# A hand-ordered two-stage kernel: the steps behind the 178th in another order, four of them on another engine

## The chip, the cores and the metric

The kernel runs on one core of a Trainium2 chip. The metric is the device time of one execution in microseconds (us); lower is better. The core has engines that each work through their own queue of instructions in order: TensorE (PE, matrix multiplication), VectorE (DVE), ScalarE (ACT), GpSimd (POOL) and SyncE (SP), which here only issues transfers. Between engines there are semaphores: an instruction waits until what it reads has been written, or until the buffer that it writes has been read for the last time.

## The reference

Attention by polynomial sketches, then a layer whose activation is a quotient of polynomials, on 4 batches of 4 heads, 1088 tokens, 32 per head:

```python
def phi(x):
    a = np.einsum('rd,bhsd->bhsr', S1, x)
    b = np.einsum('rd,bhsd->bhsr', S2, x)
    return np.einsum('bhsi,bhsj->bhsij', a, b).reshape(*x.shape[:-1], r * r)
q_p, k_p = (phi(q), phi(k))
kv = np.einsum('bhsf,bhsd->bhfd', k_p, v)
z = np.sum(k_p, axis=2)
num = np.einsum('bhsf,bhfd->bhsd', q_p, kv)
den = np.einsum('bhsf,bhf->bhs', q_p, z)[..., None] + 1e-06
...
h = x @ w_in                      # x: num / den, (4352, 128); w_in: (128, 2048)
P = a[0] + a[1] * h + a[2] * h2 + a[3] * h3
Q = 1.0 + np.abs(b[0]) * np.abs(h) + np.abs(b[1]) * h2
g = P / (Q + 1e-06)
return (g @ w_out).astype(np.float32)
```

## The kernel before

Nothing in the kernel is scheduled by the compiler: the instructions of every engine stand in the order in which the program issues them, and that is the order of the string `ORDER`, 650 steps. A loop at the end of the kernel splits each step at its points, looks up a function by its first letters and calls it; a last `.a` puts the step on ScalarE, `.d` on VectorE. Moving a step in the string moves its instructions in its engine's queue and changes when its buffers are taken. Each tile belongs to a group of a fixed number of buffers, and a new one takes a buffer whose last reader has come.

The first stage works on keys (`K`, batch.what) and queries (`Q`, batch.part.what). For keys: `T` transpose (VectorE, line 299), `s` sketches (TensorE, 306), `c` copy of one sketch out of PSUM, `f` features (VectorE, 318), `p` products with the values (TensorE, 337), `k` copy of the result (into kvz). For queries: `T` transpose, `sk` sketches (TensorE, 373), `c` copy, `dw` and `dr` write to and read back from memory (issued by SP, 399 to 410), `f` features (VectorE, 417), `p` numerator and denominator (TensorE, 433), `pl` denominator plus 1e-6 (442 on VectorE, 445 on ScalarE), `r` reciprocal (VectorE, 450), `x` quotient (VectorE, 455), `b` three transposes back (TensorE, 461), `kk` copy into xT, the second stage's input.

The second stage has 21 units, each of 256 or 512 tokens by 4, 8 or 16 blocks of 128 hidden columns; most are 128 x 4096 values, units 18 to 20 are 128 x 2048 and twice 128 x 1024. A unit's steps:

- `H` hidden layer in parts of 1024 (TensorE, 518, 32-bit) and `E` its evacuation from PSUM as bf16 into hh (line 272 on ScalarE, 274 on VectorE). Two PSUM buffers serve all H.
- the denominator: `U` absolute value (531; on ScalarE 529), `W` scale and bias (539; on ScalarE 537), `Y` product (554), all VectorE. In units 6, 8, 10, 12 and 14 ScalarE's `D` (544) takes the square instead of W and Y, and `M`, a transfer issued by GpSimd (550), joins u to it.
- `L` logarithm (ScalarE, 576) and `X` exponential (ScalarE, 581): the reciprocal r, in two buffers.
- the numerator: `P` (VectorE 559, ScalarE 562), `V` (VectorE, 572); in units 7, 9 to 15 `A` adds a constant from memory, by a transfer that GpSimd issues (568). `S` (VectorE, 585) multiplies hh and r, `G` (VectorE, 589) S and the numerator. Units 16 and 17 have `B` and `C` (594, 601) instead.
- `Or`, `Os`, `Og`, `Om`, `On` (TensorE, 618): products with the second weights, summed in one PSUM accumulator; all units of the same tokens share it. `ST` (ScalarE, 272; the last, ST20, on VectorE and ScalarE, 633 and 635) empties it, and only then can the next tokens begin. `OUT` stores (SP, 655).

`w6` and `w7` make scaled copies of the second weights for units 16 and 17, in memory that the key features k_p have left (lines 678 on VectorE, 680 on ScalarE). `F` loads the next batch's q, k or v, `AW` writes the constant for A to memory, `Z` are idle matmuls.

Of the kernel before, what the change touches and what calls it, by code (L numbers as in the profile page):

```python
# [770 lines left out]
```

## Time and profile before

| | us |
|---|---|
| median of 3 runs (254.99 to 255.8) | 255.01 |
| the profiled execution's own time | 255.07 |
| its span, first to last instruction | 253.3 |
| TensorE busy, 2603 matmuls | 244.4 |
| VectorE busy, 229 instructions | 240.1 |
| ScalarE busy, 179 instructions | 231.9 |
| GpSimd busy, 59 instructions | 32.9 |

The time is 1.8 us longer than the span; what lies around the span belongs to the program's start and end. Busy times of one engine can't be added over instructions: on VectorE and ScalarE each instruction begins a little before the one in front has ended, unless it waits for something. In lists of groups a row has line, engine, operation, out<-in with shapes, count, busy us and mean ns of one. In timelines a row has start, duration, engine, line, and in brackets idle time ahead and what ended it; equal neighbours are merged into one row.

### The profile page before, as it was taken

To read this page: it belongs to the slowest core of one execution; us is meant where nothing else is said; L and a number is where in the kernel's file an instruction comes from. 1 tells how busy PE (TensorE), PEld (TensorE's weight loads), DVE (VectorE), ACT (ScalarE), POOL (GpSimd) and SP (SyncE) were. 2 spreads that over 40 slices of the span, in tenths; PEclk is the share of its full clock that TensorE was granted. 3 is DMA by queue.
4 is the path that set the end of the run, shared out by engine and by line. 5 is a ranking of instruction groups with operands and counts; after the bars stand their busy time and mean duration, and the time that the engine had idled before them with its cause. 6 is when DMAs were issued, how large, how long until landed. Compare 5 with 4: busy or idle time off the path is not lost.

```text
span 253.3 us, 6086 instructions
## 1 busy us (share of the span) xinstructions
PE 244.4 (96%) x2603; PEld 172.1 (68%) x2606; DVE 240.1 (95%) x229; ACT 231.9 (92%) x179; POOL 32.9 (13%) x59
## 2 busy tenths in 40 slices
PE   7999899999999999999999999899999999999983
PEld 3777645665576667666676677565757589999883
DVE  3798999999999999999999999999999999999993
ACT  2179989998999999999999999999999999999990
POOL 4030000000003000420040700620125200000000
PEclk9999999999999999999999999999999999999999
DMA  6998475407925487599028992799187991000111
GB/s 180 278 333 187 146 242 179 129 6 238 215 70 114 91 185 225 115 207 194 5 63 190 177 204 42 138 161 213 30 168 129 212 211 34 0 3 3 41 47 39
DMA packets 22458, 34.47 MB, mean 136 GB/s; under 512 B 2976, under 2 KB 14880, under 8 KB 22432
## 3 DMA queue, kind: packets, MB, share of 16 engines
q0 software_dynamic: 3744, 13.63, 29.2%
q1 hardware_dynamic: 18400, 20.38, 28.8%
q8 instruction: 20, 0.33, 0.5%
q10 hardware_dynamic: 288, 0.08, 0.1%
q14 instruction: 6, 0.05, 0.1%
HBM read 25.10 MB, written 3.74 MB: 114 GB/s over the span
## 4 chain that ended last, share of the span: by engine, by line
PE 38%; ACT 21%; DVE 19%; issue 13%; DMA 6%; SPq 1%; ACTq 0%; DVEq 0%
PE h_ps L518 20%; PE out_ps L618 10%; ACT r L581 6%; ACT ln L576 6%; ACT hh L272 5%; DVE g L589 3%; DVE w L554 3%; DMA v_sb<-in_v_dram 3%; DVE s L585 3%; PE att_ps L337 3%; PE att_ps L433 2%; DVE g L594 2%; DVE g L572 2%; DMA k_sb<-in_k_dram 2%; DVE w L539 2%
## 5 line engine op out<-in xcount | busy, mean ns | idle before, releaser
L518 PE MATMUL h_ps<-xT,w_in_sb 128*128 128x512 f32 (+1 forms) x320 | 128.4, 538 | 0.2 <-DMA w_in_sb<-in_moe_w_in_dram 0.2
L518 PEld LDWEIGHTS h_ps<-xT,w_in_sb 128*128 128x128 f32 x320 | 56.8, 190 | 36.4 <-issue 31.9
L272 ACT CAST hh<-h_ps 128x1024 bf16<-128x1024 f32 x66 | 65.9, 1044 | 2.0 <-PE h_ps L518 1.9
L581 ACT ACTIVATE r<-ln 128x4096 bf16<-128x4096 f32 (+2 forms) x21 | 63.1, 3004 | 0.5 <-PE out_ps L618 0.5
L576 ACT ACTIVATE ln<-w 128x4096 f32<-128x4096 bf16 (+2 forms) x16 | 44.9, 2803 | 0.0
L585 DVE TENSOR_TENSOR s<-hh,r 128x4096 bf16<-128x4096 bf16 (+2 forms) x21 | 39.4, 1879 | 0.2 <-ACT r L581 0.2
L618 PEld LDWEIGHTS <-r 128*128 128x128 bf16 x544 | 31.8, 98 | 8.8 <-issue 8.3
L618 PEld LDWEIGHTS <-g 128*128 128x128 bf16 x544 | 31.7, 98 | 7.2 <-issue 5.6
L618 PE MATMUL out_ps<-w_out,r 128*128 128x128 bf16 x544 | 33.7, 219 | 1.5 <-ACT out_sb L272 1.5
L589 DVE TENSOR_TENSOR g<-g,s 128x4096 bf16<-128x4096 bf16 (+2 forms) x19 | 34.7, 1837 | 0.1
L572 DVE TENSOR_TENSOR g<-g,hh 128x4096 bf16<-128x4096 bf16 (+2 forms) x19 | 34.7, 1834 | 0.0
L618 PE MATMUL out_ps<-w_out,g 128*128 128x128 bf16 x480 | 29.8, 219 | 0.1
L550 POOL DMA_DIRECT2D w<-u x10 | 12.3, 1359 | 133.3 <-ACT w L544 74.2
L554 DVE TENSOR_TENSOR w<-w,u 128x4096 bf16<-128x4096 bf16 (+2 forms) x16 | 28.0, 1750 | 0.1
L618 PEld LDWEIGHTS <-s 128*128 128x128 bf16 x352 | 20.6, 98 | 5.3 <-issue 4.0
L531 DVE TENSOR_SCALAR u<-hh 128x4096 uint16<-128x4096 uint16 (+2 forms) x20 | 20.9, 1047 | 0.8 <-ACT hh L272 0.8
L576 ACT ACTIVATE ln<-w,scale 128x4096 f32<-128x4096 bf16 x5 | 18.8, 3759 | 0.0
L544 ACT ACTIVATE w<-hh,root 128x4096 bf16<-128x4096 bf16 x5 | 18.6, 3726 | 0.1
L568 POOL DMA_DIRECT2D g<-ones x16 | 15.6, 1240 | 22.7 <-DVE g L572 13.0
L559 DVE TENSOR_SCALAR g<-hh,a_k 128x4096 bf16<-128x4096 bf16 (+2 forms) x16 | 18.5, 1168 | 0.0
L618 PE MATMUL out_ps<-w_out,s 128*128 128x128 bf16 x288 | 18.2, 219 | 0.0
L539 DVE TENSOR_SCALAR w<-u,b_abs 128x4096 bf16<-128x4096 bf16 (+2 forms) x15 | 16.6, 1106 | 0.0
(92 smaller groups left out, 194.5 us busy)
## 6 DMA issues: line engine op xcount, KB each, us to landing
g<-ones POOLq DMA_DIRECT2D x16, 512.0 KB, 9.6
w<-u POOLq DMA_DIRECT2D x10, 512.0 KB, 6.0
a_all<-sk_d SPq DMA_DIRECT2D x6, 352.0 KB
b_all<-sk_d SPq DMA_DIRECT2D x12, 176.0 KB
v_sb<-in_v_dram SPq DMA_DIRECT2D x12, 144.0 KB
k_sb<-in_k_dram SPq DMA_DIRECT2D x3, 544.0 KB
q_sb<-in_q_dram SPq DMA_DIRECT2D x3, 544.0 KB
out_dram<-out_sb SPq DMA_DIRECT2D x19, 64.0 KB
```

Of the source, the lines that this page charges most:

```text
L272: nc.scalar.copy(out=out, in_=in_)
L518: nc.tensor.matmul(t[:, (x - part * m) * tl:(x - part * m + 1) * tl], lhsT=w_in_sb[:, (f0 + x) * 128:(f0 + x + 1) * 128], rhs=xT[:, p:p + ...
L531: nc.vector.tensor_scalar(out=at(i, "u", *c).bitcast(U16), in0=at(i, "hh", *c).bitcast(U16), scalar1=0x7FFF, scalar2=None, op0=AX.bitwise_and)
L539: nc.vector.tensor_scalar(out=at(i, "w", *c), in0=at(i, "u", *c), scalar1=ab1, scalar2=ab0, op0=AX.mult, op1=AX.add)
L544: nc.scalar.activation(out=at(i, "w", *c), in_=at(i, "hh", *c), func=ACT.Square, scale=root)
L554: nc.vector.tensor_mul(out=at(i, "w", *c), in0=at(i, "w", *c), in1=at(i, "u", *c))
L572: nc.vector.tensor_mul(out=at(i, "g", *c), in0=at(i, "g", *c), in1=at(i, "hh", *c))
L576: nc.scalar.activation(out=ln_sb[:, :ce - c], in_=at(i, "w", c, ce), func=ACT.Ln, bias=1.0 + 1e-6, scale=scale0 if i in SQ else 1.0)
L581: nc.scalar.activation(out=at(i, "r", c, ce), in_=ln_sb[:, :ce - c], func=ACT.Exp, scale=-1.0)
L585: nc.vector.tensor_mul(out=at(i, "s", *c), in0=at(i, "hh", *c), in1=at(i, "r", *c))
L589: nc.vector.tensor_mul(out=at(i, "g", *c), in0=at(i, "g", *c), in1=at(i, "s", *c))
L618: nc.tensor.matmul(outs[t0][:, m * 128:(m + 1) * 128], lhsT=z[:, m * 128:(m + 1) * 128], rhs=w, start=first and j == 0 and m == 0, stop=le ...
```

## The change

Only the string differs. The first 178 steps stay as they are; behind them the same steps stand in another order. Four steps have another engine: `Q2.1.pl` and `w7` go from ScalarE to VectorE, `U19` too, and `Q3.0.pl` goes from VectorE to ScalarE. GpSimd's steps keep their order among themselves; those of the four other engines change places.

```diff
-Q1.2.dw Q1.1.dr K2.s1 Q0.3.p X2.0 E4.0.a P3.1.a H4.2 Q0.3.pl.d K2.c1.d Q1.0.f Q2.0.c.a V3.0 Q0.3.r Og1.0 E4.1.a L3.0
-Q1.0.p Q1.0.pl.a H4.3 Os1.0 Q1.0.r Q0.3.x E4.2.a Q0.3.b Q1.0.x Q1.0.b Q1.2.dr Or2.0 S2.0 E4.3.a Q0.3.kk.a Q1.0.kk.a
-H5.3 X3.0 U4.0.d H5.2 E5.2.a K2.f1 Q1.1.f Q2.2.sk Q1.1.p Q1.1.pl.a G2.0 Q2.1.sk Q2.1.c.a E5.3.a Q2.0.dw W4.0.d H5.0
-Og2.0 H5.1 Q1.1.r Y4.0 E5.0.a Or1.0 L4.0 E5.1.a H6.2 Os2.0 Q1.1.x Q1.2.f S3.0 Q2.2.c.a H6.3 ST2.a E6.2.a E6.3.a F3.q
-Q1.1.b Q1.1.kk.a Q3.0.T H6.1 X4.0 Q2.1.dw H6.0 F3.k E6.0.a Q1.2.p F2.v Q1.2.pl.a K2.p0 K2.p1 Q3.2.T P4.0.d U5.0.d
-Q2.0.dr Q3.1.T W5.0.d H7.0 V4.0 Y5.0 E6.1.a D6.0 K2.k0.a Q1.2.r S4.0 K3.T2 K3.T1 Os4.0 H7.2 Q2.1.dr Or4.0 U6.0.d
-E7.0.a H7.3 L5.0 E7.2.a E7.3.a Q1.2.x Q2.0.f Q1.2.b Q3.0.sk Q3.0.c.a Q1.2.kk.a Q3.0.dw OUT2 G4.0 X5.0 K3.T0 P5.0.d
-G3.0 Q2.2.dw Q2.0.p H7.1 Q2.0.pl.d Og3.0 Q2.1.f M6.0 E7.1.a Q2.0.r L6.0 V5.0 Q2.0.x H8.3 Q2.0.b S5.0 U7.0.d P7.0.d
-H8.2 F3.v Or3.0 E8.2.a P6.0.d E8.3.a W7.0.d Q2.0.kk.a H8.0 Os3.0 H8.1 X6.0 Og4.0 E8.0.a V6.0 Y7.0 S6.0 Q3.0.dr H9.0
-E8.1.a D8.0 U8.0.d M8.0 Q3.1.sk E9.0.a Q3.1.c.d K3.s0 Q2.1.p Q2.1.pl.a Q3.2.sk Q2.2.dr Q2.2.f AW0 K3.c0.d ST4.a Q3.0.f
-H9.1 Q2.1.r P8.0.d V7.0 A7.0 L7.0 Or6.0 E9.1.a Q2.1.x G6.0 X7.0 H9.2 G5.0 Os6.0 S7.0 E9.2.a H9.3 E9.3.a U9.0.d K3.f0
-Or5.0 L8.0 H10.3 Q2.1.b Q2.1.kk.a E10.3.a H10.0 E10.0.a Q3.1.dw W9.0.d V8.0 Og6.0 X8.0 H10.1 E10.1.a Y9.0 G7.0
-Q3.2.c.d S8.0 H10.2 Og5.0 E10.2.a U10.0.d D10.0 M10.0 Q3.1.dr Q3.1.f H11.0 E11.0.a Os5.0 P9.0.d K3.s1 K3.c1.d Q2.2.p
-Q2.2.pl.d P10.0.d ST6.a Q2.2.r V10.0 H11.1 L9.0 Or8.0 H11.3 OUT4 Q2.2.x Q2.2.b K3.f1 E11.1.a V9.0 X9.0 H11.2 K3.p0
-E11.2.a K3.p1 H12.1 Or7.0 S9.0 K3.k0.d Q3.2.dw E11.3.a U11.0.d OUT6 w6.d W11.0.d Y11.0 L10.0 A9.0 E12.1.a X10.0 H12.0
-E12.0.a L11.0 Q3.1.p G8.0 A10.0 Q3.0.p Q3.0.pl.d H12.2 Os8.0 H12.3 E12.2.a E12.3.a Og8.0 Q3.2.dr Q3.1.pl.d Q2.2.kk.a
-D12.0 Q3.1.r Q3.0.r Q3.1.x Q3.0.x G9.0 S10.0 Q3.0.b Q3.0.kk.d Og7.0 w7.a U12.0.d M12.0 ST8.a OUT8 H13.0 E13.0.a H13.1
-E13.1.a P12.0.d Or9.0 P11.0.d V12.0 A12.0 V11.0 H13.2 X11.0 Q3.1.b Q3.1.kk.a H13.3 Q3.2.f G10.0 E13.2.a Or10.0 E13.3.a
-S11.0 L12.0 U13.0.d H14.1 E14.1.d Q3.2.p Q3.2.pl.a H14.2 W13.0.d Q3.2.r E14.2.d Q3.2.x X12.0 Y13.0 S12.0 H14.0 E14.0.a
-H14.3 Q3.2.b E14.3.a Q3.2.kk.a Og9.0 U14.0.d H15.2 D14.0 P13.0.d E15.2.a Og10.0 ST10.a L13.0 G12.0 P14.0.d A11.0 G11.0
-M14.0 Z4 V13.0 A13.0 H15.3 Or12.0 E15.3.a V14.0 H15.0 H15.1 X13.0 Og11.0 E15.1.a S13.0 E15.0.a Or11.0 U15.0.d H16.0
-L14.0 H16.1 P15.0.d E16.0.a E16.1.a X14.0 Og12.0 ST12.a H16.3 E16.3.a W15.0.d H16.2 E16.2.a OUT12 V15.0 Y15.0 S14.0
-L15.0 U16.0.d Or13.0 G13.0 H17.3 W16.0.d H17.1 E17.3.a A14.0 Or14.0 E17.1.a G14.0 X15.0 H17.2 E17.2.a Y16.0 S15.0
-H17.0 E17.0.a U17.0.d OUT10 W17.0.d Og14.0 A15.0 L16.0 Og13.0 ST14.a G15.0 X16.0 H18.1 Y17.0 S16.0 H18.0 E18.0.a
-E18.1.a U18.0.d Or15.0 L17.0 X17.0 Og15.0 Or16.0 B16.0 W18.0.d C16.0 Y18.0 Os16.0 H19.0 Om16.0 E19.0.a U19.0.a On16.0
-ST16.a H20.0 OUT16 S17.0 Os17.0 B17.0 Om17.0 C17.0 P18.0.a W19.0.a Y19.0 L18.0 E20.0.a P19.0.d On17.0 X18.0 L19.0
-V18.0 Or17.0 ST17.a U20.0.d V19.0 W20.0.d Y20.0 S18.0 Or18.0 X19.0 Or19.0 S19.0 G19.0 G18.0 OUT17 Os18.0 Og19.0
-P20.0.a V20.0 Os19.0 Og18.0 L20.0 X20.0 Or20.0 S20.0 G20.0 OUT14 Os20.0 Og20.0 ST20 OUT20
+Q1.2.dw Q1.1.dr K2.s1 Q0.3.p X2.0 E4.0.a P3.1.a H4.2 Q0.3.pl.d K2.c1.d Q1.0.f Q2.0.c.a E4.1.a Og1.0 Q0.3.r V3.0 Q1.0.p
+Q0.3.x L3.0 Q1.0.pl.a Q1.2.dr H4.3 E4.2.a Os1.0 Q1.0.r E4.3.a Q1.0.x Q0.3.b Q0.3.kk.a Q1.0.b Or2.0 S2.0 U4.0.d
+Q1.0.kk.a H5.2 K2.f1 Q1.1.f W4.0.d X3.0 Q2.0.dw H5.3 E5.3.a G2.0 Q2.1.sk F2.v Q2.2.sk Q2.1.c.a F3.q E5.2.a Q1.1.p Y4.0
+Q2.2.c.a Q1.1.pl.a Q1.1.r H5.0 E5.0.a Og2.0 L4.0 H5.1 Q1.2.f Or1.0 H6.2 Q1.1.x S3.0 E5.1.a Os2.0 ST2.a E6.2.a P4.0.d
+Q3.1.T H6.3 Q1.1.b E6.3.a X4.0 Q1.1.kk.a H6.0 E6.0.a U5.0.d H6.1 Q3.0.T Q3.0.sk Q2.1.dw Q3.0.c.a W5.0.d E6.1.a K2.p0
+K2.p1 K2.k0.a D6.0 Q1.2.p V4.0 Y5.0 S4.0 F3.k K3.T2 K3.T1 H7.0 K3.T0 E7.0.a U6.0.d G3.0 M6.0 Q1.2.pl.a Os4.0 H7.2
+Or4.0 L5.0 E7.2.a H7.3 Q2.0.dr Q2.0.f Q2.0.p Q1.2.r Q2.1.dr Q2.1.f Q3.0.dw Q1.2.x X5.0 P5.0.d Q3.0.dr Q2.2.dw Q1.2.b
+Q1.2.kk.a E7.3.a H7.1 Og3.0 G4.0 Q2.0.pl.d Q3.2.T E7.1.a Q2.0.r H8.3 V5.0 Q2.0.x Q2.0.b S5.0 L6.0 H8.2 E8.2.a U7.0.d
+E8.3.a F3.v Or3.0 Q2.0.kk.a P6.0.d W7.0.d P7.0.d H8.0 V6.0 Os3.0 X6.0 Y7.0 E8.0.a S6.0 H8.1 E8.1.a U8.0.d D8.0 Q2.2.dr
+OUT2 Og4.0 ST4.a H9.0 Q3.1.sk Q3.1.c.d Q2.2.f Q2.1.p Q2.1.pl.d K3.s0 K3.c0.d Q2.1.r Q3.2.sk Q3.2.c.d E9.0.a H9.1 Or6.0
+L7.0 M8.0 Q2.1.x Q2.1.b K3.f0 H9.2 E9.1.a X7.0 E9.2.a Os6.0 H9.3 E9.3.a V7.0 AW0 Or5.0 P8.0.d H10.3 G6.0 L8.0 G5.0
+S7.0 U9.0.d E10.3.a W9.0.d H10.0 E10.0.a V8.0 Q3.1.dw Y9.0 Og6.0 X8.0 H10.1 H10.2 Og5.0 E10.1.a A7.0 G7.0 E10.2.a
+Q2.1.kk.a H11.0 Q3.1.dr Q3.1.f Os5.0 S8.0 D10.0 Q2.2.p E11.0.a U10.0.d P9.0.d K3.s1 Q2.2.pl.d ST6.a Q3.2.dw H11.1
+Or8.0 Q3.0.f OUT6 Q2.2.r H11.2 K3.c1.d Q2.2.x L9.0 E11.1.a P10.0.d Q2.2.b K3.f1 V9.0 M10.0 V10.0 X9.0 E11.2.a H11.3
+E11.3.a S9.0 K3.p0 K3.p1 w7.d U11.0.d w6.d L10.0 W11.0.d H12.1 E12.1.a Or7.0 H12.0 K3.k0.d Q3.0.p Q3.1.p X10.0 Y11.0
+Q3.1.pl.d H12.2 Q3.0.pl.a G8.0 E12.0.a L11.0 E12.2.a Q3.0.r Os8.0 A9.0 H12.3 E12.3.a Q3.1.r Og8.0 Q3.0.x Q3.0.b Og7.0
+Q3.1.x G9.0 Q2.2.kk.a S10.0 A10.0 Q3.0.kk.d H13.0 D12.0 Q3.1.b Q3.1.kk.a U12.0.d ST8.a M12.0 P12.0.d H13.1 E13.1.a
+Q3.2.dr P11.0.d E13.0.a Or9.0 X11.0 H13.3 Q3.2.f V12.0 G10.0 V11.0 S11.0 H13.2 E13.3.a E13.2.a U13.0.d Or10.0 H14.1
+E14.1.d L12.0 OUT4 Q3.2.p W13.0.d Q3.2.pl.a Q3.2.r H14.2 E14.2.d H14.0 X12.0 E14.0.a H14.3 Q3.2.x Q3.2.b Y13.0 E14.3.a
+Q3.2.kk.a H15.2 D14.0 S12.0 U14.0.d A12.0 G12.0 E15.2.a Og10.0 Og9.0 ST10.a P14.0.d Z4 H15.3 P13.0.d L13.0 A11.0
+Or12.0 G11.0 V14.0 V13.0 E15.3.a X13.0 S13.0 H15.1 Og11.0 E15.1.a H15.0 E15.0.a Or11.0 M14.0 U15.0.d L14.0 H16.1
+P15.0.d W15.0.d OUT8 E16.1.a H16.0 E16.0.a Og12.0 X14.0 H16.3 ST12.a E16.3.a V15.0 OUT10 Y15.0 H16.2 S14.0 E16.2.a
+Or13.0 U16.0.d A13.0 OUT12 G13.0 W16.0.d H17.3 H17.1 L15.0 Og13.0 E17.3.a A14.0 G14.0 Y16.0 E17.1.a X15.0 H17.0
+E17.0.a S15.0 H17.2 E17.2.a U17.0.d L16.0 W17.0.d Og14.0 Or14.0 ST14.a A15.0 G15.0 H18.0 X16.0 Y17.0 S16.0 H18.1
+E18.1.a E18.0.a Or15.0 U18.0.d B16.0 W18.0.d C16.0 Og15.0 H19.0 L17.0 X17.0 Os16.0 E19.0.a Y18.0 S17.0 Or16.0 Om16.0
+L18.0 On16.0 ST16.a U19.0.d H20.0 OUT14 W19.0.a P19.0.d B17.0 V19.0 Or17.0 C17.0 X18.0 Y19.0 P18.0.a V18.0 OUT16
+E20.0.a U20.0.d Os17.0 S18.0 L19.0 W20.0.d X19.0 Om17.0 On17.0 S19.0 ST17.a Y20.0 Or18.0 Or19.0 Os19.0 Os18.0 G19.0
+P20.0.a G18.0 Og19.0 Og18.0 L20.0 X20.0 Or20.0 V20.0 OUT17 S20.0 G20.0 Os20.0 Og20.0 ST20 OUT20
```

## The prediction

> **What bounds the kernel now.** I read the page's first part, then the chain that ended last, then busy time by stretches.
>
> ```profile
> PE 244.4 (96%) x2603; PEld 172.1 (68%) x2606; DVE 240.1 (95%) x229; ACT 231.9 (92%) x179; POOL 32.9 (13%) x59
> PE 38%; ACT 21%; DVE 19%; issue 13%; DMA 6%; SPq 1%; ACTq 0%; DVEq 0%
> ```
> ```profile
> 106.00:142.00 36.00, 36.00 (x390) 24.46 (x388) 36.00 (x28) 35.97 (x22) 7.43 (x9) 1.00 0.66 140
> 142.00:163.00 21.00, 20.24 (x233) 14.41 (x232) 20.72 (x19) 20.93 (x13) 5.28 (x6) 1.00 0.68 126
> 163.00:205.00 42.00, 41.74 (x349) 26.81 (x349) 41.34 (x27) 41.86 (x27) 10.77 (x11) 1.00 0.84 157
> 205.00:249.50 44.50, 43.31 (x575) 40.17 (x574) 43.51 (x34) 42.13 (x27) 0.00 (x0) 1.00 0.17 40
> ```
>
> Three engines are full at once. In the stretches (columns: length, then busy us of TensorE, its weight loads, VectorE, ScalarE, GpSimd, then clock, DMA share, GB/s) none of the three is idle between 106 and 142 us, and VectorE is idle for 0.28, 0.66 and 0.99 us in the three stretches behind. The clock is whole, so it plays no part. An order adds and removes no operation. It can win only waits, and for every wait that goes the two other engines must be able to come earlier too. Opening and first 178 steps stay, so I look behind 46 us only.
>
> Busy time hides one half of what a wait costs. VectorE's timeline shows it (start, duration, engine and line, in brackets the idle time in front):
>
> ```profile
> 209.17 2.29 DVE L589 TENSOR_TENSOR g<-g,s 128x4096 bf16<-128x4096 bf16 x1
> 211.37 2.29 DVE L554 TENSOR_TENSOR w<-w,u 128x4096 bf16<-128x4096 bf16 x1
> ...
> 231.81 2.29 DVE L585 TENSOR_TENSOR s<-hh,r 128x4096 bf16<-128x4096 bf16 x1
> 234.13 2.29 DVE L594 TENSOR_TENSOR g<-s,hh 128x4096 bf16<-128x4096 bf16 x1
> 236.53 2.29 DVE L601 TENSOR_TENSOR s<-g,hh 128x4096 bf16<-128x4096 bf16 x1
> 238.74 0.69 DVE L554 TENSOR_TENSOR w<-w,u 128x1024 bf16<-128x1024 bf16 x1
> ```
>
> Two multiplications that don't depend on each other start 2.20 us apart though each lasts 2.29: the next begins 0.09 before the end of the last. S17, B17 and C17, each of which reads what the one before wrote, start 2.32 and 2.40 apart. So a wait costs its idle time and 0.08 to 0.09 of lost overlap, and I count in distances between starts.
>
> **The change part by part: VectorE's ledger.** First the waits that the new order takes away.
>
> ```profile
> 143.20 1.34 DVE L539 TENSOR_SCALAR w<-u,b_abs 128x4096 bf16<-128x4096 bf16 x1
> 144.57 2.29 DVE L554 TENSOR_TENSOR w<-w,u 128x4096 bf16<-128x4096 bf16 x1
> ...
> 152.66 2.29 DVE L585 TENSOR_TENSOR s<-hh,r 128x4096 bf16<-128x4096 bf16 x1
> 155.16 0.56 DVE L274 COPY xT<-att_ps 128x384 f32<-128x384 f32 x1 [0.21 <-PE att_ps L461]
> ...
> 170.52 1.23 DVE L274 CAST hh<-h_ps 128x1024 bf16<-128x1024 f32 x1 [0.30 <-PE h_ps L518]
> ...
> 173.28 1.23 DVE L274 CAST hh<-h_ps 128x1024 bf16<-128x1024 f32 x1 [0.15 <-PE h_ps L518]
> ...
> 202.26 2.29 DVE L585 TENSOR_TENSOR s<-hh,r 128x4096 bf16<-128x4096 bf16 x1 [0.18 <-ACT r L581]
> 204.57 1.23 DVE L531 TENSOR_SCALAR u<-hh 128x4096 uint16<-128x4096 uint16 x1
> ...
> 241.87 0.54 DVE L539 TENSOR_SCALAR w<-u,b_abs 128x1024 bf16<-128x1024 bf16 x1
> 242.45 0.69 DVE L554 TENSOR_TENSOR w<-w,u 128x1024 bf16<-128x1024 bf16 x1
> 243.06 1.82 DVE L585 TENSOR_TENSOR s<-hh,r 128x2048 bf16<-128x2048 bf16 x2
> 244.91 1.83 DVE L589 TENSOR_TENSOR g<-g,s 128x1024 bf16<-128x1024 bf16 x2
> ```
>
> - W11 to Y11, 1.37 for 1.25 (its duration less 0.09): 0.12. K3.k0 now stands between them.
> - S10 to the copy Q3.0.kk, 2.50 for 2.20: 0.30. The copy waits for TensorE's Q3.0.b, an instant that doesn't move; VectorE will reach it 0.66 later (w7, below) and find it done.
> - The two evacuations of unit 14 on VectorE, 0.30 + 0.15 idle and 0.16 of overlap: 0.61. They wait for H14.1 and H14.2, which come earlier (below), while VectorE comes later.
> - Y15 to S14 to U16: 0.18 + 0.08, and 2.31 for 2.20: 0.37. S14 waits for the reciprocal of unit 14 from ScalarE.
> - S17 to B17 to C17: 0.12 + 0.20 = 0.32. U19, P19 and V19 now stand between.
> - W20 to Y20, 0.58 for 0.46, and S18 with S19 to G19, 1.85 for 1.73 (1.82 less 0.09): 0.12 each, 0.24. S19 and Y20 now stand between.
>
> Together 1.96. Then what VectorE takes over:
>
> ```profile
> 158.57 2.06 ACT L680 ACTIVATE k_p<-w_out,a_k 128x2048 bf16<-128x2048 bf16 x1
> ```
> ```profile
> L678 DVE TENSOR_SCALAR k_p<-w_out,a_k 128x2048 bf16<-128x2048 bf16 x1 | 0.7, 747 | 0.0
> ...
> L531 DVE TENSOR_SCALAR u<-hh 128x1024 uint16<-128x1024 uint16 x3 | 1.3, 425 | 0.8 <-ACT hh L272 0.8
> ```
>
> w7, 2.06 on ScalarE, costs VectorE what its twin w6 costs: 0.747 less 0.08, 0.66. U19 costs 0.425 less 0.09, 0.34. Q2.1.pl comes to VectorE and Q3.0.pl leaves it: nothing. W9 now follows U9, whose result it reads: 0.12, as above. Together 1.12, and the ledger says 1.96 - 1.12 = **0.84 less**. Some pairs that win or lose 0.1 each I leave out; I set them against each other.
>
> Between 46 and 106 us I count nothing either way. At its end VectorE copies the sketches Q3.1, K3 and Q3.2 from PSUM just as TensorE makes them, and TensorE has no wait to give up before Or9 (below); what VectorE wins in front of them it loses there.
>
> **Do the other two follow?** ScalarE is rid of w7 and U19, but it can't use all of it:
>
> ```profile
> 161.16 1.95 PE L618 MATMUL out_ps<-w_out,r 128*128 128x128 bf16 x32 [0.76 <-ACT out_sb L272]
> ```
> ```profile
> 163.14 3.62 ACT L581 ACTIVATE r<-ln 128x4096 bf16<-128x4096 f32 x1 [0.21 <-PE out_ps L618]
> ...
> 166.66 0.43 ACT L272 COPY xT<-att_ps 128x352 f32<-128x352 f32 x1
> ...
> 168.80 3.73 ACT L576 ACTIVATE ln<-w,scale 128x4096 f32<-128x4096 bf16 x1
> ```
> ```profile
> 164.71 0.49 PE L461 MATMUL att_ps<-ident,x_tok 128*128 128x128 f32 x3
> ```
> ```profile
> 198.53 3.70 ACT L581 ACTIVATE r<-ln 128x4096 bf16<-128x4096 f32 x1
> ```
>
> TensorE's Or9 waits 0.76 for ST8, which stands behind w7 on ScalarE and empties the only accumulator. Without w7, ST8 is done before TensorE gets there. But X11 waits for Or9, which reads the buffer that X11 writes, and Or9 still has H13.1 and now Q3.1.b in front, three transposes of 0.49 in all (last row but one), some 0.4 with overlap. So Or9 begins near 161.16 - 0.76 - 0.1 + 0.4 = 160.7 and X11 near 162.6: 0.5 of w7's 2.06 is won, the rest becomes a wait for H13.1, as E13.1 now stands ahead of E13.0. Q3.1.kk (0.43, 0.33 without overlap) leaves the place behind X11, so L12 starts 0.8 earlier, at 168.0. That shift carries on to X14: 198.53 - 0.8 + 3.70 is 201.4. VectorE, with 1.03 won (the first three terms) and 0.78 added (w7, W9) by then, could start S14 at 202.00 - 0.25, 201.75, and finds it ready. U19 is taken off ScalarE near the end, so there ScalarE comes earlier still. TensorE has its waits for ScalarE (0.76 here) to give up and doesn't hold it back. The profiled execution took 255.07 us; 255.07 - 0.84 = **254.2 us**. The median of the runs is 255.01, so this is 0.8 us or 0.3% under it.
>
> **Moved work and queues.** K3.k0 now comes behind w7, U11, w6 and W11.
>
> ```profile
> 141.20 0.29 DVE L274 COPY kvz<-att_ps 128x132 f32<-128x132 f32 x1
> ```
> ```profile
> 145.90 1.63 PE L433 MATMUL att_ps<-kvz,a_all 128*64 128x66 f32 x48
> ```
>
> TensorE reads at 145.90 what it writes. W11's start of 143.20 less the 0.2 that K3.k0 no longer takes in front, plus w7's 0.66, W9's 0.12, W11's 1.25 and K3.k0's own 0.29 give its end, 145.3: a margin of 0.6, and nothing is charged. GpSimd's queue keeps its order. On SP's queue OUT2 goes behind Q2.2.dr, OUT4 behind Q3.2.dr, F2.v ahead of F3.q: the loads come no later, and a store ends nothing here but OUT20. The waits of Q3.0.dr for Q2.0.f hold up only loads whose users come 15 us later.
>
> **A rule against the change.** GpSimd writes the descriptors of the joins (M) and of the additions of a1 (A).
>
> ```profile
> 139.61 5.01 POOL L568 DMA_DIRECT2D g<-ones  x4 [6.80 <-DVE g L572]
> ```
> ```profile
> L568 POOL DMA_DIRECT2D g<-ones x16: 861/1100/3397, 108.8 to 200.9; - x16
> ```
> ```profile
> L550 POOL DMA_DIRECT2D w<-u x10: 855/1204/2327, 77.3 to 183.0; - x10
> ...
> DMA to landing us min/median/max: 4.5/6.0/9.5
> ```
>
> Four issues take 5.01 us at 139.61, though the shortest takes 0.86, and the longest of all, 3.40, is among them: it must lie near the end of these four, under VectorE's U11, w6 and W11 (the last from 143.20 to 144.54). The Trainium skill, "SBUF — State Buffer", section "Who interferes with whom", says that a VectorE tensor_scalar in its fast mode locks GpSimd out of a shared port, so that descriptors aren't written until it ends; the trace agrees. By that rule w7, one tensor_scalar more, would hold A10 back longer, 0.66 at most. Row by row the answer is nothing: A10's data are used at 162, 20 us later.
>
> The join of unit 12 is where a late descriptor would hurt. The last fence holds the joins: each issue takes 0.86 to 2.33, and they land 4.5 to 9.5 us behind it, 6.0 by the median. D12 ends near 158.4 (0.2 ahead of w7's start in before), while VectorE does P12 and P11 until about 159.6; issued then, the join lands at 164 to 169, 166 by the median. L12 wants it at 168.0.
>
> **The rivals.**
> - *The waits only move* (25%). If X11 or L12 gains nothing, ScalarE keeps its old times up to X14 and VectorE waits for it at S14 as before, however early it comes. Then only the end counts: 0.32 + 0.24 - 0.34 = 0.2 less, **254.9**. For it: ScalarE's part of the chain and 35.97 of 36.00 busy; against it: ST8 and Q3.1.kk do leave ScalarE's path.
> - *Slower: the join of unit 12 lands late* (18%). Issued at 159.6 to 161.4 and with the longest landing, 9.5, it comes at 169.1 to 170.9, L12 is up to 2.1 later than in before (168.80), and all of ScalarE behind it; less the 0.2 of the end, up to 1.9 more, 257.0; at 170.0 it is **256.1**. It decides once the join lands after 169.8. Against it: the median of 6.0.
> - *All waits go* (12%). 1.93 idle behind 106, less the 0.71 below, and eighteen lost overlaps of 0.09 (the places that VectorE's timeline shows), are 2.8; less w7 and U19 **253.2**.
>
> ```profile
> 249.43 0.29 DVE L633 COPY out_sb<-out_ps 128x128 f32<-128x128 f32 x1 [0.71 <-PE out_ps L618]
> ```
>
> - *It doesn't do what it says*: the same 650 steps stand in both orders, four on another engine, so this can be only the first rival under another name.
>
> **How the numbers follow.** The forecast has 45%, with 253.6 to 254.5 as its own range. This measurement can tell about 0.3%, 0.77 us, from no change: faster is under 254.25, slower over 255.8. Two thirds of the forecast's 45 and the 12 of the case that all waits go give 0.42 for faster; the other third and 23 of the first rival's 25 give 0.38 for no change; the join's 18 and the 2 left of the first rival give 0.20 for slower. The range leaves out half of each outer case and holds the rest: 253.2 to 256.2.
>
> **What would show it.** Right: no idle bracket ahead of the copy at 155, of unit 14's evacuations and of S14; L12 near 168.0, S14 near 201.75; the end of VectorE's work 0.8 earlier; ScalarE idle near 160. Wrong: X11 still at 163.1; L12 waiting for a DMA; a wait ahead of TensorE's Q3.0.p near 146; VectorE idle at the sketches near 102 to 104, which it now reads as they are made.

## The result and the profile after

The changed kernel takes 254.43 us (median of 20 runs, 253.84 to 255.39), the kernel before, run beside it on the same chip, 255.46 (20 runs, 254.63 to 256.74). The ratio is 0.9957 with a 95% interval of 0.9946 to 0.9968: 1.1 us or 0.43% faster. The profiled execution took 254.41 us with a span of 252.6; that of before took 255.07 with 253.3.

The page's first part and its chain of waits, after:

```profile
PE 244.7 (97%) x2606; PEld 171.9 (68%) x2606; DVE 240.3 (95%) x231; ACT 229.2 (91%) x177; POOL 31.2 (12%) x59
DVE 45%; PE 33%; issue 11%; DMA 6%; ACT 2%; SPq 1%; POOL 0%; DVEq 0%; ACTq 0%
```

ScalarE's busy time fell by 2.7 us, as w7 and U19 left it. VectorE's rose by only 0.2 though it does 1.2 us more: overlapped time counts once, and each wait that went brought an overlap of 0.09 back. In the chain that ended last ScalarE fell from 21% to 2%, and VectorE rose from 19% to 45%. Busy time by stretches, after (length, then TensorE, weight loads, VectorE, ScalarE, GpSimd, clock, DMA share, GB/s):

```profile
106.00:142.00 36.00, 36.00 (x392) 24.69 (x391) 35.96 (x26) 36.00 (x22) 7.03 (x8) 1.00 0.64 124
142.00:163.00 21.00, 21.00 (x237) 14.97 (x236) 21.00 (x21) 19.77 (x15) 1.79 (x2) 1.00 0.71 156
163.00:205.00 42.00, 41.95 (x347) 26.56 (x346) 41.99 (x26) 41.98 (x27) 13.61 (x12) 1.00 0.79 152
205.00:248.80 43.80, 42.59 (x574) 39.74 (x572) 43.02 (x35) 40.94 (x26) 0.00 (x0) 1.00 0.21 46
```

VectorE's idle 0.28, 0.66 and 0.99 us of the last three stretches are 0.00, 0.01 and 0.78 now, TensorE's 0.76 and 0.26 are 0.00 and 0.05. The idle time between 142 and 163 has moved to ScalarE, 1.23.

**Counting without the opening.** Executions of one kernel differ by about a microsecond, mostly in the opening, ahead of everything that the change touches: in the fourteen traces S1 starts at 34.30 to 36.17 us. So I count from start to start on VectorE: S1 (in the opening), S6, S14, and the last G. The distances come from the trace's nanoseconds, so the last digit can differ by one from what the rows give. S14 of before stands in the prediction; the others, before and then after (start, duration, engine and line):

```profile
34.54 0.68 DVE L585 TENSOR_TENSOR s<-hh,r 128x1024 bf16<-128x1024 bf16 x1
...
99.20 2.29 DVE L585 TENSOR_TENSOR s<-hh,r 128x4096 bf16<-128x4096 bf16 x1
...
248.02 0.69 DVE L589 TENSOR_TENSOR g<-g,s 128x1024 bf16<-128x1024 bf16 x1
```
```profile
34.77 0.69 DVE L585 TENSOR_TENSOR s<-hh,r 128x1024 bf16<-128x1024 bf16 x1
...
99.14 2.29 DVE L585 TENSOR_TENSOR s<-hh,r 128x4096 bf16<-128x4096 bf16 x1
101.34 1.23 DVE L531 TENSOR_SCALAR u<-hh 128x4096 uint16<-128x4096 uint16 x1
102.82 0.34 DVE L274 COPY sk_sb<-att_ps 128x176 f32<-128x176 f32 x1 [0.25 <-PE att_ps L373]
...
141.69 0.76 DVE L678 TENSOR_SCALAR k_p<-w_out,a_k 128x2048 bf16<-128x2048 bf16 x1
142.36 1.23 DVE L531 TENSOR_SCALAR u<-hh 128x4096 uint16<-128x4096 uint16 x1
...
145.41 0.30 DVE L274 COPY kvz<-att_ps 128x132 f32<-128x132 f32 x1
145.62 2.29 DVE L554 TENSOR_TENSOR w<-w,u 128x4096 bf16<-128x4096 bf16 x1
...
155.79 0.55 DVE L274 COPY xT<-att_ps 128x384 f32<-128x384 f32 x1
...
170.71 1.21 DVE L274 CAST hh<-h_ps 128x1024 bf16<-128x1024 f32 x1
...
173.22 1.16 DVE L274 CAST hh<-h_ps 128x1024 bf16<-128x1024 f32 x1
...
201.87 2.29 DVE L585 TENSOR_TENSOR s<-hh,r 128x4096 bf16<-128x4096 bf16 x1
204.17 1.23 DVE L531 TENSOR_SCALAR u<-hh 128x4096 uint16<-128x4096 uint16 x1
...
231.43 2.28 DVE L585 TENSOR_TENSOR s<-hh,r 128x4096 bf16<-128x4096 bf16 x1
233.63 0.42 DVE L531 TENSOR_SCALAR u<-hh 128x1024 uint16<-128x1024 uint16 x1
233.97 0.54 DVE L559 TENSOR_SCALAR g<-hh,a_k 128x1024 bf16<-128x1024 bf16 x1
234.42 2.29 DVE L594 TENSOR_TENSOR g<-s,hh 128x4096 bf16<-128x4096 bf16 x1
...
247.39 0.69 DVE L589 TENSOR_TENSOR g<-g,s 128x1024 bf16<-128x1024 bf16 x1
```

| us | S1 to S6 | S6 to S14 | S14 to last G | sum |
|---|---|---|---|---|
| before | 64.66 | 103.06 | 45.76 | 213.48 |
| after | 64.36 | 102.73 | 45.52 | 212.61 |
| difference | -0.30 | -0.33 | -0.24 | -0.87 |

From S1 on the change wins 0.87 us. The two profiled times differ by 0.66 because the opening of this execution ran 0.23 later. How far such distances can be trusted shows in the table of the experiments: where the front is the same, S1 to S6 comes out alike to 0.01 us from one execution to the next (with one exception, told there), while the whole time scatters by a microsecond.

The brackets of the prediction's list are gone: nothing waits ahead of the copy at 155.79, the evacuations at 170.71 and 173.22, and S14 at 201.87. ScalarE, after:

```profile
159.73 0.59 ACT L272 COPY out_sb<-out_ps 128x512 f32<-128x512 f32 x1
161.10 1.93 ACT L272 CAST hh<-h_ps 128x1024 bf16<-128x1024 f32 x2 [0.78 <-PE h_ps L518]
162.92 3.63 ACT L581 ACTIVATE r<-ln 128x4096 bf16<-128x4096 f32 x1
...
168.23 3.75 ACT L576 ACTIVATE ln<-w,scale 128x4096 f32<-128x4096 bf16 x1
```
```profile
198.19 3.64 ACT L581 ACTIVATE r<-ln 128x4096 bf16<-128x4096 f32 x1
```

ST8 at 159.73 has w7 no longer in front. ScalarE now waits 0.78 for H13.1, X11 comes at 162.92, L12 at 168.23, X14 at 198.19. X14 ends at 201.83, and S14, which reads it, begins 0.04 later, 2.20 behind the start of the multiplication in front: VectorE and ScalarE reach this point together.

### The profile page after: what moved, and what is told of

It reads as the page before. It is cut to its first block, busy times and chain, and to the rows that moved or that the text cites. A ratio compares the mean times of both kernels' runs of the same rounds, so it can differ in the third digit from the quotient of the medians.

```text
span 252.6 us, 6102 instructions
## 1 busy us (share of the span) xinstructions
PE 244.7 (97%) x2606; PEld 171.9 (68%) x2606; DVE 240.3 (95%) x231; ACT 229.2 (91%) x177; POOL 31.2 (12%) x59
## 4 chain that ended last, share of the span: by engine, by line
DVE 45%; PE 33%; issue 11%; DMA 6%; ACT 2%; SPq 1%; POOL 0%; DVEq 0%; ACTq 0%
PE h_ps L518 18%; PE out_ps L618 9%; DVE g L589 7%; DVE g L572 7%; DVE w L554 5%; DVE s L585 5%; DVE u L531 4%; DMA w<-u 4%; DVE g L559 4%; DVE w L539 3%; DMA v_sb<-in_v_dram 2%; PE att_ps L433 2%; DVE g L594 2%; PE att_ps L337 2%; DVE a_all L417 1%
## 5 line engine op out<-in xcount | busy, mean ns | idle before, releaser
L272 ACT CAST hh<-h_ps 128x1024 bf16<-128x1024 f32 x66 | 66.6, 1047 | 3.3 <-PE h_ps L518 2.8
L550 POOL DMA_DIRECT2D w<-u x10 | 9.3, 1026 | 131.0 <-ACT w L544 111.6
L568 POOL DMA_DIRECT2D g<-ones x16 | 16.8, 1452 | 26.2 <-DVE g L572 8.6
## 6 DMA issues: line engine op xcount, KB each, us to landing
g<-ones POOLq DMA_DIRECT2D x16, 512.0 KB, 10.4
```

The lines of the kernel that those rows point to most:

```text
L272: nc.scalar.copy(out=out, in_=in_)
```

## Experiments

The theory: three engines are full at once; the change wins VectorE's waits behind 106 us, by filling them with w7 and by other neighbours at the end, and ScalarE can follow because w7 leaves it. The rivals: the gain comes from the end alone, from the front alone, from the engine moves without the order, or from the order without the engine moves. All are measured against before on the same chip; the columns are as above, and "sum" is the difference of S1 to last G from before's 213.48. The ratio is not the quotient of the two medians and can differ from it by 0.25% (e9); medians of rows with another before beside them can't be compared.

| kernel | median us (before beside it) | ratio, 95% interval | S1 to S6 | S6 to S14 | S14 to last G | sum |
|---|---|---|---|---|---|---|
| after | 254.43 (255.46) | 0.9957, 0.9946 to 0.9968 | 64.36 | 102.73 | 45.52 | -0.87 |
| e1 engines alone | 260.51 (255.44) | 1.0201, 1.0160 to 1.0242 | 64.67 | 107.04 | 46.86 | +5.09 |
| e2 order alone | 256.94 (255.44) | 1.0070, 1.0044 to 1.0097 | 64.37 | 105.00 | 46.01 | +1.90 |
| e3 end alone | 255.21 (255.44) | 0.9991, 0.9969 to 1.0014 | 64.66 | 103.06 | 45.50 | -0.25 |
| e4 front of before | 254.45 (255.44) | 0.9957, 0.9931 to 0.9983 | 64.67 | 102.35 | 45.48 | -0.98 |
| e5 Q3.0.pl alone | 257.87 (255.74) | 1.0100, 1.0069 to 1.0131 | 64.67 | 105.33 | 45.65 | +2.17 |
| e6 w7 and U19 alone | 256.25 (255.74) | 1.0026, 1.0002 to 1.0050 | 65.65 | 102.63 | 46.75 | +1.55 |
| e7 w7 back | 255.53 (255.74) | 0.9996, 0.9978 to 1.0014 | 64.37 | 103.47 | 45.51 | -0.14 |
| e8 end of before | 255.42 (255.74) | 0.9982, 0.9965 to 0.9999 | 64.37 | 102.71 | 45.76 | -0.64 |
| e9 three steps in gaps | 254.73 (256.29) | 0.9964, 0.9941 to 0.9988 | 64.37 | 102.71 | 45.51 | -0.89 |
| e10 Q3.2.kk moved | 255.20 (256.29) | 0.9978, 0.9954 to 1.0003 | 64.37 | 103.63 | 45.35 | -0.13 |
| e11 e9 and e10 | 255.09 (256.29) | 0.9966, 0.9939 to 0.9992 | 64.37 | 103.23 | 45.34 | -0.55 |
| e12 w7 and the end | 255.06 (255.88) | 0.9968, 0.9938 to 0.9998 | 64.67 | 102.64 | 45.38 | -0.79 |

**e1, the engines alone.** Before's order, with the four steps on after's engines.

```diff
-K3.s0 Q2.1.p Q2.1.pl.a Q3.2.sk
+K3.s0 Q2.1.p Q2.1.pl.d Q3.2.sk
...
-A10.0 Q3.0.p Q3.0.pl.d H12.2
+A10.0 Q3.0.p Q3.0.pl.a H12.2
...
-Q3.0.kk.d Og7.0 w7.a U12.0.d
+Q3.0.kk.d Og7.0 w7.d U12.0.d
...
-Om16.0 E19.0.a U19.0.a On16.0
+Om16.0 E19.0.a U19.0.d On16.0
```

> The order of before, but w7, U19 and Q2.1.pl on VectorE and Q3.0.pl on ScalarE, as in after. Theory (VectorE's ledger: an order wins the waits that it takes from VectorE, less the work that VectorE takes over, and only as far as ScalarE's reciprocal for S14 comes earlier too): w7 and U19 cost VectorE 1.0 us; the waits that go are those ahead of unit 14's evacuations (0.61), at S14 and behind it (0.37), because ST8 no longer stands behind w7 and X11 starts some 0.9 us earlier; 0.1 us under before, between 0.3 under and 0.2 over. Rival (the relief of ScalarE, 2.9 us of work, is the gain and the order adds little): at least 0.8 us under before.

Measured: 5.1 us slower, far from the theory. The trace of e1, ScalarE and then VectorE:

```profile
150.36 3.63 ACT L576 ACTIVATE ln<-w 128x4096 f32<-128x4096 bf16 x1
153.88 0.18 ACT L445 ACTIVATE den<-att_ps 128x12 f32<-128x12 f32 x1
```
```profile
154.09 0.23 DVE L450 RECIPROCAL rec<-den 128x12 f32<-128x12 f32 x1 [3.40 <-ACT den L445]
```

Q3.0.pl takes 0.18 us on ScalarE, but it stands behind L11 there, a logarithm of 3.63. VectorE stands still for 3.40 until it comes. I had counted only the step's length. Q2.1.pl, which costs as little, makes VectorE wait too, as it stands ahead of Q2.2.f there (e1, VectorE):

```profile
103.97 0.17 DVE L442 TENSOR_SCALAR den<-att_ps 128x12 f32<-128x12 f32 x1 [0.81 <-PE att_ps L433]
```

**e5, Q3.0.pl alone** asks whether that one step is the cause.

```diff
-A10.0 Q3.0.p Q3.0.pl.d H12.2
+A10.0 Q3.0.p Q3.0.pl.a H12.2
```

> The order of before, with one step given to the other engine: Q3.0.pl (0.17 us of VectorE) goes to ScalarE, at its old place. Theory: what the four engine moves without the order lost (5.1 us) came from this step, which on ScalarE stands behind L11, so that the quotient of Q3.0 and all behind it come 3.4 us later: slower by 3 to 5 us, 258.4 to 260.4, with VectorE waiting more than 3 us ahead of Q3.0.r. Rival: it came from w7 and U19, 1.0 us more of VectorE: then this one lies within 0.5 us of before.

Measured: 2.2 us slower from S1, all of it between S6 and S14; VectorE's wait is there.

```profile
152.85 0.23 DVE L450 RECIPROCAL rec<-den 128x12 f32<-128x12 f32 x1 [3.67 <-ACT den L445]
```

The rival falls. The size is under the theory's 3 to 5: S10 comes 3.65 later than in before, counted from S1, but S14 only 2.27, since before has waits of its own between them (0.30, 0.61 and 0.26 of the prediction's list and 0.10 ahead of S11, 1.27 together), which an already late VectorE no longer has; the last 0.1 is instructions that ran a little shorter. So Q3.0.pl makes some 2.3 of e1's 5.1. Another 1.1 is the end, with U19 (e6). For the rest there are the 0.8 of Q2.1.pl's wait and, in this execution, some 1.7 of TensorE at half clock (last section), less what w7 wins (0.4, e6); these parts come to 5.5, so some of them lie beside each other, which was not taken apart.

**e6, w7 and U19 alone**, at before's places.

```diff
-Q3.0.kk.d Og7.0 w7.a U12.0.d
+Q3.0.kk.d Og7.0 w7.d U12.0.d
...
-Om16.0 E19.0.a U19.0.a On16.0
+Om16.0 E19.0.a U19.0.d On16.0
```

> The order of before, with w7 and U19 given to VectorE at their old places, both pl steps left where they were. Theory: VectorE does 1.0 us more where before it had waits of 0.3 to 0.6 us behind w7's place (the evacuations of unit 14, S14), and TensorE's wait of 0.76 for ST8 goes; by the ledger w7 uses up the waits behind it and U19 costs its 0.34 near the end: between 0.4 under before and 0.4 over it. Rival: an engine move without its order costs several us whichever step it is: 2 us or more over before.

Measured: 0.26% or 0.7 us slower. The profiled execution was the slowest of its runs: in its opening VectorE waits 1.33 us for a transfer, hence the 65.65, which no edit touches. Behind it the two steps part. S14 comes 0.43 earlier: the brackets at unit 14's evacuations and at S14 are gone, and w7's 0.66 takes up part of them. The end loses 0.99, because U19 on VectorE now waits for ScalarE's E19 (e6, VectorE):

```profile
234.70 0.43 DVE L531 TENSOR_SCALAR u<-hh 128x1024 uint16<-128x1024 uint16 x1 [0.73 <-ACT hh L272]
```

Neither side was right as a whole: w7 alone wins, U19 alone loses three times what it takes.

**e2, the order alone**: after's order with the four steps on before's engines.

```diff
-Q2.1.p Q2.1.pl.d K3.s0
+Q2.1.p Q2.1.pl.a K3.s0
...
-K3.p1 w7.d U11.0.d
+K3.p1 w7.a U11.0.d
...
-H12.2 Q3.0.pl.a G8.0
+H12.2 Q3.0.pl.d G8.0
...
-ST16.a U19.0.d H20.0
+ST16.a U19.0.a H20.0
```

> The order of after, but the four steps on their old engines, so that w7 stands on ScalarE between E11 and L10 and U19 between E19 and L18. Theory: ScalarE is 2.3 us later at L10; some 1.4 us of that vanishes in its waits ahead of Q3.1.kk and E13.1, the rest reaches X14, so S14 comes 0.9 us later than in after, and the 0.66 us that VectorE is spared can't be used; behind S14 it keeps the 0.34 us of U19. About 0.4 us under before, between 0.8 under and level. Rival of the relief: level with before. A third view, that the order alone is the gain: 1.0 us under before, as after.

Measured: 1.5 to 1.9 us slower, against an expected gain. After's order puts w7 ahead of L10. On ScalarE it takes 2.00 us there, at 142.00, and D12 behind it ends later. So the join of unit 12 is issued at 162.50, 3.3 later than in after (159.22), though the opening ran only 1.3 later. Its second half, issued at 163.0, also took 8.7 us to land, where after's took 7.4, and L12 waits for it (e2, ScalarE, then the landings):

```profile
142.00 2.00 ACT L680 ACTIVATE k_p<-w_out,a_k 128x2048 bf16<-128x2048 bf16 x1
...
171.84 3.71 ACT L576 ACTIVATE ln<-w,scale 128x4096 f32<-128x4096 bf16 x1 [1.34 <-DMA w<-u]
```
```profile
DMA to landing us min/median/max: 5.3/7.0/8.7
```

Counted from S1, X11 comes 0.86 later than in after, near the expected 0.9, but L12 2.30 and S14 2.27. The join, which the expectation left out, makes the difference. Without the longer landing its data would have been there at 170.4, just about when L12 could have started. This is the prediction's slower rival, met in another kernel.

**e7, w7 back on ScalarE**, everything else as after.

```diff
-K3.p1 w7.d U11.0.d
+K3.p1 U11.0.d
...
-H13.0 D12.0 Q3.1.b
+H13.0 D12.0 w7.a Q3.1.b
```

> The order and the engines of after, but w7 on ScalarE again and right behind D12, where before has it. Theory: ScalarE does 2.06 us more ahead of ST8 and X11 and wins back only the 0.78 that it waits for H13.1, so X11 and all behind it up to X14 come about 1.2 later, S14 waits for its reciprocal 1.2 longer less the 0.66 that VectorE gains: 0.6 to 1.2 us over after. Rival: ScalarE has slack there and w7's engine doesn't matter: within 0.2 us of after, or 0.5 faster by w7's time on VectorE.

Measured: S6 to S14 0.74 longer than after, within the theory's 0.6 to 1.2; the whole time is before's again (0.9996). S14 waits for ScalarE (e7, VectorE):

```profile
202.88 2.29 DVE L585 TENSOR_TENSOR s<-hh,r 128x4096 bf16<-128x4096 bf16 x1 [0.23 <-ACT r L581]
```

**e3 and e8, the end.** e3 has before's first 578 steps and after's last 72, with U19 on VectorE; e8 has after's first 578 and before's last 72.

```diff
-Y17.0 S16.0 H18.0 E18.0.a E18.1.a U18.0.d Or15.0 L17.0
...
+Y17.0 S16.0 H18.1 E18.1.a E18.0.a Or15.0 U18.0.d B16.0
...
```

> The first 578 steps as in before (they are the same set in both orders, up to G15 near 218 us), the last 72 as in after, U19 on VectorE among them. Theory: only the pairs at the end count, 0.32 at S17, B17 and C17 and 0.24 at W20 and S19, less 0.34 for U19: 0.2 us under before. Rival (the gain arises at the end, because there alone nothing can swallow it): 0.8 us or more under before.

> The first 578 steps of after, then the last 72 (from about 218 us on) in the order and on the engines of before, U19 on ScalarE again. The counterpart of the run with the new end alone. Theory: the end is worth 0.2 (0.32 and 0.24 of waits won, 0.34 for U19 lost), the rest lies ahead: 0.2 over after, 0.8 under before. Rival: the end is worth nothing by itself because in before ScalarE, and not VectorE's queue, sets it; then this kernel, whose VectorE comes earlier, gives back more than 0.5.

Measured: the end is worth 0.25 in e3, 0.24 as the difference of e8 and after, and the two sums, -0.25 and -0.64, make after's -0.87. So over a quarter of the gain arises at the end and the rest ahead of it; the rival falls. The medians of e8 and after lie further apart, but their intervals overlap.

**e4, the front of before**: the first 320 steps of after's order in before's sequence, the rest as after.

```diff
-E4.1.a Og1.0 Q0.3.r V3.0 Q1.0.p
+V3.0 Q0.3.r Og1.0 E4.1.a L3.0
...
```

> The 320 steps that come first in after (up to S6, near 100 us) in the order that they have in before, the rest as in after. Theory: between 46 and 106 us nothing is won, as VectorE is held there by TensorE, which has no wait: as after, 1.0 us under before within 0.3. Rival (part of the gain is the earlier loads and the pairs in front, F2.v ahead of F3.q, Q0.3.r ahead of V3): 0.5 us under before or less.

Measured: as fast as after, so the new front wins nothing. After gains 0.30 up to S6 and gives it back at once (counted from S1, S14 even comes 0.07 later than in e4): its copy of sketch Q3.1 waits 0.25 idle (102.82, above), 1.48 behind U8. In e4 (VectorE) the same two stand 1.13 apart, without a wait.

```profile
101.83 1.22 DVE L531 TENSOR_SCALAR u<-hh 128x4096 uint16<-128x4096 uint16 x1
102.96 0.33 DVE L274 COPY sk_sb<-att_ps 128x176 f32<-128x176 f32 x1
```

**e9, e10 and e11: does a wait that is left still cost?** e9 moves three VectorE steps into gaps of after, e10 gives Q3.2.kk, between X11 and X14 on ScalarE, to VectorE, e11 does both.

```diff
-D8.0 Q2.2.dr OUT2 Og4.0 ST4.a H9.0 Q3.1.sk Q3.1.c.d Q2.2.f
+D8.0 Q2.2.dr OUT2 Og4.0 ST4.a H9.0 Q3.1.sk Q2.2.f Q3.1.c.d
...
-U9.0.d E10.3.a W9.0.d H10.0 E10.0.a V8.0
+U9.0.d V8.0 E10.3.a W9.0.d H10.0 E10.0.a
...
-Y11.0 Q3.1.pl.d H12.2 Q3.0.pl.a G8.0
+Y11.0 G8.0 Q3.1.pl.d H12.2 Q3.0.pl.a
```
```diff
-E14.3.a Q3.2.kk.a H15.2 D14.0 S12.0 U14.0.d
+E14.3.a H15.2 D14.0 S12.0 Q3.2.kk.d U14.0.d
```

> After with three VectorE steps moved into the gaps that are left ahead of S14: Q2.2.f ahead of the copy Q3.1.c (VectorE waits 0.25 us there for the sketches), V8 between U9 and W9 which depends on it, G8 ahead of Q3.1.pl which reads what is late. VectorE's queue could come 0.55 us earlier to S14 (0.34 + 0.12 + 0.09). Theory: S14 starts 0.04 us behind the end of X14 on ScalarE, so ScalarE's chain from X11, held by TensorE's H13.1, sets it: VectorE's gain becomes a wait at S14, and the time stays within 0.15 us of after. Rival, VectorE's ledger alone: 0.5 under after.

> After with one step moved: Q3.2.kk, a copy of 0.54 us on ScalarE between X11 and X14, goes to VectorE behind S12. ScalarE's chain up to X14 gets 0.5 shorter, VectorE's up to S14 some 0.3 longer. Theory: both end together at S14 in after (0.04 us apart), so the longer of the two sets it: 0.2 to 0.4 over after. Rival, ScalarE alone sets the pace: 0.3 to 0.5 under after.

> After with both edits: the three VectorE steps in the gaps (0.55 earlier at S14) and Q3.2.kk given to VectorE (0.3 later there, ScalarE 0.5 earlier). Theory: only together do they bring S14 forward, VectorE by 0.25 and ScalarE by 0.5: 0.2 to 0.3 under after. Rival, VectorE's ledger alone: as the kernel with the three steps moved but 0.3 slower. Rival, something else ahead of S14 is late (TensorE's transposes, unit 14's hidden layer): no gain over after.

Measured: e9 nothing (-0.89 for -0.87), e10 0.74 slower than after, e11 0.32 slower. e9 doesn't carry as much as it was meant to: the wait for the sketches only goes to the next copy, and W9 to Y9 becomes the dependent pair, so that of 0.55 just 0.09 is won, and S14 waits exactly that long for X14. That fits the theory but tests it weakly. In e10 the copy costs VectorE 0.62 (two instructions), not the 0.3 that I had taken, and ScalarE's 0.54 is lost as waits for TensorE. First VectorE in e10, then ScalarE:

```profile
147.92 0.17 DVE L442 TENSOR_SCALAR den<-att_ps 128x12 f32<-128x12 f32 x1 [0.27 <-PE att_ps L433]
```

```profile
191.88 1.01 ACT L272 CAST hh<-h_ps 128x1024 bf16<-128x1024 f32 x1 [0.27 <-PE h_ps L518]
```

VectorE's wait at 147.92 lies ahead of the edit, and so does its cause. In this execution the join of unit 8 landed 10.4 us behind its issue (9.5 in after), and L8 waited for it on ScalarE:

```profile
114.59 3.72 ACT L576 ACTIVATE ln<-w,scale 128x4096 f32<-128x4096 bf16 x1 [0.19 <-DMA w<-u]
```

ScalarE is late from there on, TensorE waits 0.18 for it at 125.79 and runs 0.28 later behind S1 than in after, and VectorE meets that at the products: 0.27 of e10's longer S6 to S14, beside the copy's 0.62, is not the edit's. In e11, where nothing of the kind happens, S6 to S14 is 0.49 longer. There X14 starts 163.41 us behind S1, in after 163.42, though ScalarE has the copy no more: it waits 0.27 for TensorE ahead of E15.0, as in e10. So what holds S14's reciprocal is not ScalarE by itself but TensorE, idle for 0.05 us of after's stretch of 42. e11's theory falls with that, and the rival that something else ahead of S14 is late comes true: ScalarE can't come earlier, VectorE comes 0.5 later.

**e12, w7 and the end**: before's first 578 steps with w7 on VectorE, after's last 72.

```diff
-Q3.0.kk.d Og7.0 w7.a U12.0.d
+Q3.0.kk.d Og7.0 w7.d U12.0.d
...
-Y17.0 S16.0 H18.0 E18.0.a E18.1.a U18.0.d Or15.0 L17.0
+Y17.0 S16.0 H18.1 E18.1.a E18.0.a Or15.0 U18.0.d B16.0
...
```

> The first 578 steps of before with one change, w7 given to VectorE at its old place, then the last 72 steps of after with U19 on VectorE. In the kernel with w7 and U19 moved in the order of before, S14 came 0.43 us earlier behind S6, and U19 then lost 0.99 because VectorE waited for its data; with the new end alone, the end won 0.26. Theory: the parts add up, S6 to S14 0.43 shorter and S14 to the last G 0.26 shorter, 0.7 together against the 0.87 of the whole change: 0.2 over after. Rival: U19 needs all of the new order, not only that of the end, so that a wait of some 0.7 us stays ahead of U19 and the end is longer than in before.

Measured: -0.42 and -0.38, 0.79 of the 0.87. U19 stands without a wait here (e12, VectorE):

```profile
231.93 2.29 DVE L585 TENSOR_TENSOR s<-hh,r 128x4096 bf16<-128x4096 bf16 x1
234.13 0.42 DVE L531 TENSOR_SCALAR u<-hh 128x1024 uint16<-128x1024 uint16 x1
```

The rival falls: U19 needs the new end, with S17 ahead of it, and nothing more. w7 on another engine and 72 steps in a new order, U19 among them, bring nine tenths of the gain; the other new places behind the 178th step and the two pl bring 0.08. w7's move does two things at once: X14 starts 0.54 earlier behind S1 than in before, and VectorE's waits take up the 0.66. e7 shows that the first is needed; what the second alone is worth, no run shows. By the trace e4, 0.1 under after, would be the fastest of all; by the medians it can't be told from after.

## The prediction, point by point

The forecast, 254.2 us, was right in direction, in size and in mechanism: 0.84 less was predicted and 0.87 measured from S1 on; the medians say 1.1, with an interval of 0.8 to 1.4 (0.32 to 0.54% of 255.46). That the two sums agree to 0.03 is luck: two misses of 0.1 cancel.

- **The waits that go.** All on the list went but one: S14 to U16 is still 2.30 for 2.20. The prediction put this place down to the reciprocal, but U16 waits for something else, the evacuation E16.2, which ScalarE ends at 204.14 (before: 204.54), 0.03 ahead of U16 in both kernels:

```profile
202.18 1.96 ACT L272 CAST hh<-h_ps 128x1024 bf16<-128x1024 f32 x2
```

A new wait of 0.09 stands behind Y11, where Q3.1.pl wants TensorE's products just as they are done (147.87, see K3.k0). Up to S14 the prediction had 0.51 less (201.75 for 202.26); S1 to S14 is 0.63 shorter. Behind it, 0.33 by its terms, the 0.11 at U16 among them; 0.24 was measured.

- **The work added.** w7 took 0.67 (141.69 to 142.36; predicted 0.66), U19 0.34 (233.63 to 233.97; predicted 0.34).
- **46 to 106 us, nothing either way.** Right, for the reason given: 0.30 won ahead of the sketches and lost at them; e4 shows it. One of the signs that were to show it wrong did come, VectorE idle at the sketches (0.25 at 102.82), but it cost little more than what had been won in front.
- **ScalarE follows.** X11 at 162.6, L12 at 168.0, r ready at 201.4 and S14 at 201.75 were predicted; 162.92, 168.23, 201.83 and 201.87 were measured, in an execution that had begun 0.23 later. The prediction had the reciprocal ready 0.35 ahead of VectorE; it was ready 0.04 ahead, so ScalarE only just follows. That TensorE doesn't hold it back was too easy: by e10 and e11 it is TensorE that keeps the reciprocal from coming earlier. e7 shows that w7's leaving is what lets ScalarE follow at all.
- **K3.k0.** Its end was put at 145.3 and came at 145.71; TensorE starts the products that read it at 146.24 without a wait:

```profile
146.24 1.63 PE L433 MATMUL att_ps<-kvz,a_all 128*64 128x66 f32 x48
```

- **"Q2.1.pl comes to VectorE and Q3.0.pl leaves it: nothing."** True only of the whole change, and my reason for it was too weak: in before's order the first makes VectorE wait 0.8 (e1) and the second costs 2.3 (e5), by the place where they stand in the queue. In after's order Q3.0.pl stands ahead of L11.
- **The rival that the waits only move** was refuted by the brackets that are gone. **That all go**, 253.2, did not come: of what was left some waits only changed their places (e9) and others are for TensorE (e10, e11).
- **The rule against the change**, that w7 holds A10 back, was not put to the test. In after A10's two issues end at 141.86, 0.17 behind w7's start, and none of the four of A9 and A10 took over 1.23 us (3.40 in before):

```profile
140.10 1.76 POOL L568 DMA_DIRECT2D g<-ones  x2 [0.42 <-issue]
```

- **The late join.** In after the joins land 4.7 and 7.4 us behind their issues, which start at 159.2 and 160.1, so by 167.5: 0.7 ahead of L12. The row (after, landing of these two):

```profile
DMA to landing us min/median/max: 4.7/6.1/7.4
```

The margin was thin, as e2 shows, where L12 waits 1.34 for the same join.
- **What the prediction did not see**: that its ledger needs little of the new order. w7 in its old place fills the same waits (e12).

## What to carry to other kernels

When several engines are full at once, a short step that is given to another engine can cost what stands in front of it in that queue, not its own length: here 0.18 us of work cost 2.3 us. A wait can be filled only where the work for it is at hand: w7, which reads nothing that is late, won 0.43 by itself; U19, which had to wait for its data, lost 0.99. To tell changes of a few tenths from a scatter of one microsecond, measure between two fixed instructions of the trace, see that the parts add up, and look for what differs ahead of the edit (e10).
